# Score tiles of 512 columns in one PSUM bank each, w_out's first piece fetched earlier, and new orders of both stages

## The chip, the cores and the metric

The kernel runs on one core of one Trainium2 chip. The metric is device time in microseconds (us) of one execution, the median of several runs; lower is better. Engines are named as in the profile: PE is TensorE's matmul, PEld its weight load, DVE is VectorE, ACT is ScalarE, POOL is GpSimd, and SP is SyncE, which here only issues DMAs.

## The reference

Three layers follow each other, all in fp32. First bucketed attention: B, H, S, D = 2, 8, 768, 64, and a key counts for a query only where both fall in the same of 64 hash buckets.

```python
q_bits = (np.einsum('bhsd,dk->bhsk', q, proj) > 0); k_bits = ...      # 6 bits
mask = q_bucket[:, :, :, None] == k_bucket[:, :, None, :]
scores = np.where(mask, scale * np.matmul(q, k.transpose(0, 1, 3, 2)), -1e9)
attn = np.exp(scores - scores.max(-1, keepdims=True))
out = np.matmul(attn / (attn.sum(-1, keepdims=True) + 1e-09), v)
```

Then a soft mixture of experts over the 1536 tokens (x is 1536x512, phi 512x32, 8 experts, w1 512x1024, w2 1024x512):

```python
logits = x @ phi
d = softmax(logits, axis=0); c = softmax(logits, axis=1)
slot_input = d.T @ x                                  # 32 slots, 4 for each expert
slot_out[e] = np.maximum(slot_input[e] @ w1[e], 0) @ w2[e]
x = c @ slot_out
```

Last a feed-forward layer: `h = x @ w_in; g = h - np.tanh(h); return g @ w_out`, with w_in 512x2048 and w_out 2048x512. The weights arrive as fp64 and the kernel converts w_in and w_out to fp32 itself.

## The kernel before, in words

**Stage 1, attention (0 to about 263 us).** The 16 heads are worked in 8 pairs (NPR). What each engine does, and in what order, is written out by hand: START lists the units of the beginning, STEP those of one pair (run for pairs 0 to 6), LAST those of pair 7. A unit's name is looked up in `units`, and `role` says for which pair it is done: `m` and `f2` for the next pair, `b` and `h` for the one after it, `s0`, `s1`, `a` for the pair itself, `x2`, `x3`, `lg` for the one before.

- `m` (m_unit, L405) takes 128 queries and all 768 keys of one head: two matmuls (512 and 256 columns) write one PSUM tile `pm`, and DVE takes the row maximum (L412). There are 6 for a head. `f2`, `fa`, `fb` (m_fin) turn the maxima into a row that is added into the scores.
- `s0`, `s1` (s_unit, L461) do 128 keys against all 768 queries of head 0 or 1: four matmuls (L465 and L467, hi and lo parts) write one PSUM tile `pst`, ACT takes the exponential into an SBUF tile `e` (L469), and POOL adds it to the running sum `es` (L474, L480). There are 6 for a head.
- `a` (av_unit, L483) multiplies the two heads' `e` by v into the PSUM tiles `pav` (L492).
- `xr` sums `es` over the partitions with a matmul by ones (L503), `xe` copies `pav` out, `x2` takes the reciprocals, `x3` and `lg` make the tokens and their logits.

All those PSUM tiles (`pm`, `pst`, `pc`, `pb`, `pr`, `pl`, `px` and others) come out of one pool `ps` of three tiles of 768 columns, taken in turn: a new tile waits until the tile three places back has been read. 768 fp32 columns are 3 KB, one bank is 2 KB, so each tile takes two banks. `pav` has two further banks. The `e` tiles are 8 of 768 columns.

**Weights.** `pieces` is the order in which 1 MB pieces are fetched: 32 of w1 and w2, then slots (which = 4, without a DMA) that will hold the converted w_out, and w_out's raw pieces (which = 3). RING says how many slots of SBUF are opened at each of eight points, as buffers of the attention come free; `lp` and `load_pieces` issue the next pieces.

**Stage 2, MOE and feed-forward (263 us to the end).** MOE lists the units of the mixture of experts and of the preparation of the feed-forward layer: `F`, `X`, `y` read the weights, `k` and `i` are matmuls whose result is not used (keep_clock, L748), `ca` to `ce` convert a block f of w_out (ACT L174, DVE L178, L187, L192, ACT L1111, POOL L1112), `m q g s S` make the n-th block of g, `r` and `ra`/`rv` copy the product of the slots with w_in to all rows (L1014, then ACT L1023 or DVE L1021). After MOE all engines load a flag and branch (L1293, L1294); then RUN is worked through, in which `u` stands for three matmuls of 512 columns into an output tile (L1217 to L1219), and a loop (LOOP, LOOP2) does the rest.

Of the kernel before, what the change touches and what calls it, by code (L numbers as in the profile page):

```python
# [10 lines left out]
F32 = mybir.dt.float32  # L11
# [12 lines left out]
NB = 6  # L24
# [103 lines left out]
def body(ctx: ExitStack, tc: tile.TileContext, q, k, v, proj, phi, w1, w2, w_in, w_out, cst, out, dbg=None):  # L128
# [113 lines left out]
    def attention():  # L242
# [9 lines left out]
        e_p = pool("e_p", 8)  # L252
# [11 lines left out]
        ps = actx.enter_context(tc.tile_pool(name="ps", bufs=3, space=PSUM, reuse_waits="tile"))  # L264
# [37 lines left out]
        def psum(name):  # L302
            return ps.tile([P, S], F32, tag="s", name=name)
# [39 lines left out]
        def bits0(i, which):  # L343
            x = (xqs, xks)[which][i]
            pb = psum("pb")
            bt0[which] = e_p.tile([P, S], F32, tag="e", name="bt0")[64:64 + 4 * NB]
            for c0, c1 in ((0, 512), (512, S)):
                nc.tensor.matmul(pb[64:96, c0:c1], projb, x[:, c0:c1], start=True, stop=True, tile_position=(0, 64))  # L348
            for c0, c1 in ((0, 512), (512, S)):
                nc.vector.tensor_scalar(bt0[which][:, c0:c1], pb[64:64 + 4 * NB, c0:c1], 0.0, None, ALU.is_gt)  # L350

        def rows0(i, which, h, eng):
# [3 lines left out]
            for c0, c1, e in {"s": ((0, 512, "a"), (512, S, "v"))}.get(eng, ((0, S, eng),)):  # L356
                y, b = X[i][h][rs, c0:c1], bt0[which][:, c0:c1]
# [47 lines left out]
        def m_unit(i, n):  # L405
            s, h, c = i % 3, n // KT, n % KT
            if i not in mx:
                mx[i] = pre.tile([P, 2 * KT], F32, tag="mx", name="mx")
            pm = psum("pm")
            for c0, c1 in ((0, 512), (512, S)):  # L410
                nc.tensor.matmul(pm[:, c0:c1], QA[s][h][:96, c * P:(c + 1) * P], KA[s][h][:96, c0:c1], start=True, stop=True)  # L411
            nc.vector.reduce_max(mx[i][:, h * KT + c:h * KT + c + 1], pm, axis=AX.X)  # L412

        def m_fin(i, hs=(0, 1)):
            s, n = i % 3, len(hs)
            pc = psum("pc")
            m = pc[:n * KT, :P]
            nc.tensor.transpose(m, mx[i][:, hs[0] * KT:(hs[-1] + 1) * KT], ident)
# [42 lines left out]
        def s_unit(i, h, c):  # L461
            s, t = i % 3, i % 2
            pst = psum("pst")
            for c0, c1 in ((0, 512), (512, S)):
                nc.tensor.matmul(pst[:, c0:c1], KA[s][h][:, c * P:(c + 1) * P], QA[s][h][:, c0:c1], start=True, stop=False)  # L465
            for c0, c1 in ((0, 512), (512, S)):
                nc.tensor.matmul(pst[:, c0:c1], KB[t][h][:, c * P:(c + 1) * P], QB[t][h][:, c0:c1], start=False, stop=True)  # L467
            e = e_p.tile([P, S], F32, tag="e", name="e")
            nc.scalar.activation(e, pst, AF.Exp, scale=0.125)  # L469
            if c == 0:  # L470
                es[i, h, 0] = e
            elif c == 1:
# [873 lines left out]
```

## Time and profile before

| | |
|---|---|
| median of 3 runs | 472.83 us (472.68 to 473.65) |
| profiled execution: time, span | 473.9 us, 472.0 us |
| mean granted clock of PE | 0.984 |
| PE busy | 452.9 us, 96% of the span |
| DVE busy | 325.4 us, 69% |
| POOL busy | 297.5 us, 63% |
| ACT busy | 256.7 us, 54% |

Busy time is the union of an engine's instructions in the trace. Matmuls overlap each other in the records, so a PE that shows 99% busy can still have lost time between two of them; the idle time in front of a weight load, with what ended it, tells more. The windows of the stage table cut the span into the start (13 to 45), the pairs (about 29 us each), the last pair and the tail (235 to 263) and the mixture of experts (263 to 319).

### The profile page before, as it was taken

What the parts mean: (1) busy time and instruction counts of PE and PEld (TensorE: products, weight loads), DVE (VectorE), ACT (ScalarE), POOL (GpSimd) and SP (SyncE); (2) the same over time, 40 slices, a digit from 0 to 9 for tenths busy, and PEclk for the clock granted to TensorE, in tenths of its full rate; (3) what the DMA queues carried; (4) which work ended last, traced back from release to release, by engine and by line L of the source; (5) the groups of instructions that cost most, each with busy time, mean ns of one, the idle gap of its engine ahead of it and who ended that gap; (6) DMA issues with size and microseconds to landing.
All of it is one profiled execution on the core that took longest, in us unless ns stands there. A gap on an engine that the chain in (4) does not pass through costs nothing.

```text
span 472.0 us, 7262 instructions
## 1 busy us (share of the span) xinstructions
PE 452.9 (96%) x2589; PEld 295.7 (63%) x2589; DVE 325.4 (69%) x496; ACT 256.7 (54%) x441; POOL 297.5 (63%) x247
## 2 busy tenths in 40 slices
PE   7799999999999999999999999979999999999995
PEld 3455555655656565565675444547777778888883
DVE  3999688897878969658253658078999976545441
ACT  3434655646556555453452111177798977656661
POOL 3979978789787988679972100025788885353440
PEclk9889999999999999999999999997999999999999
DMA  6337174362834517459589999990000003000003
GB/s 199 109 103 223 56 206 119 104 183 62 231 86 140 145 53 235 183 173 315 228 331 393 316 396 421 419 419 26 1 1 0 0 2 134 2 0 1 0 0 140
DMA packets 18898, 72.66 MB, mean 154 GB/s; under 512 B 3780, under 2 KB 4904, under 8 KB 13736
## 3 DMA queue, kind: packets, MB, share of 16 engines
q1 hardware_dynamic: 18536, 72.12, 44.1%
q8 instruction: 22, 0.36, 0.3%
q14 instruction: 20, 0.16, 0.1%
q10 hardware_dynamic: 320, 0.01, 0.0%
HBM read 60.08 MB, written 3.15 MB: 134 GB/s over the span
## 4 chain that ended last, share of the span: by engine, by line
PE 86%; DVE 8%; ACT 3%; issue 1%; DMA 1%; POOL 0%; SPq 0%; DVEq 0%; ACTq 0%; POOLq 0%
PE pav L492 14%; PE po L1219 9%; PE po L1217 9%; PE po L1218 9%; PE pst L465 8%; PE pm L411 8%; PE pst L467 7%; DVE mx L412 3%; PE po L902 3%; PE ph L1155 2%; PE po L926 2%; PE pl L562 2%; PE pr L503 1%; PE pb L348 1%; ACT e L469 1%; PE px L548 1%
## 5 line engine op out<-in xcount | busy, mean ns | idle before, releaser
L480 POOL TENSOR_TENSOR es<-es,e 128x768 f32<-128x768 f32 x59 | 114.0, 1946 | 13.7 <-ACT e L469 13.5
L469 ACT ACTIVATE e<-pst 128x768 f32<-128x768 f32 x96 | 76.4, 809 | 81.5 <-PE pst L467 77.1
L412 DVE TENSOR_REDUCE mx<-pm 128x1 f32<-128x768 f32 x96 | 87.6, 951 | 13.6 <-PE pm L411 12.5
L492 PE MATMUL pav<-e,tv 128*64 128x256 f32 (+1 forms) x384 | 70.7, 496 | 0.0
L411 PE MATMUL pm<-KA,QA 96*128 96x512 f32 x192 | 53.6, 380 | 5.4 <-DVE mx L412 2.1
L1167 DVE SCALAR_TENSOR_TENSOR ph<-win,ph 128x512 f32<-128x512 f32 x64 | 35.7, 557 | 33.4 <-ACT win L1162 32.2
L465 PE MATMUL pst<-QA,KA 128*128 128x512 f32 x192 | 54.9, 367 | 1.0 <-ACT e L469 0.9
L1198 POOL TENSOR_TENSOR split<-win,split 128x512 fp32r<-128x512 f32 x31 | 44.6, 1440 | 14.1 <-ACT split L1193 12.8
L1219 PE MATMUL po<-w,split 128*128 128x512 f32 x128 | 51.8, 405 | 0.2 <-POOL split L1198 0.2
L1217 PE MATMUL po<-w,split 128*128 128x512 f32 x128 | 51.3, 401 | 0.0
L1218 PE MATMUL po<-w,split 128*128 128x512 f32 x128 | 51.1, 399 | 0.0
L467 PE MATMUL pst<-QB,KB 128*128 128x512 f32 x192 | 49.3, 338 | 0.0
L1198 POOL TENSOR_TENSOR ghl<-win,ghl 128x256 fp32r<-128x256 f32 x32 | 24.4, 763 | 38.4 <-ACT ghl L1193 38.4
L492 PEld LDWEIGHTS pav<-e,tv 128*64 128x64 f32 x384 | 24.5, 136 | 38.1 <-issue 36.4
L411 PEld LDWEIGHTS pm<-KA,QA 96*128 96x128 f32 x192 | 29.5, 192 | 29.4 <-ACT e L469 10.3
L474 POOL TENSOR_TENSOR es<-e 128x768 f32<-128x768 f32 x16 | 34.5, 2159 | 20.0 <-ACT e L469 19.9
L1162 ACT ACTIVATE win<-ph 128x512 f32<-128x512 f32 (+1 forms) x64 | 30.8, 481 | 24.7 <-PE ph L1155 24.0
L1168 DVE SCALAR_TENSOR_TENSOR win<-win,ph 128x512 f32<-128x512 f32 x64 | 35.5, 554 | 8.3 <-ACT win L1163 0.2
L1163 ACT ACTIVATE win<-win,ct 128x512 f32<-128x512 f32 (+1 forms) x64 | 39.5, 617 | 2.1
L465 PEld LDWEIGHTS pst<-QA,KA 128*128 128x128 f32 x192 | 29.0, 189 | 14.3 <-issue 6.4
L467 PEld LDWEIGHTS pst<-QB,KB 128*128 128x128 f32 x192 | 29.4, 188 | 4.2
L1219 PEld LDWEIGHTS po<-w,split 128*128 128x128 f32 x128 | 24.4, 191 | 8.2 <-POOL split L1198 3.0
(233 smaller groups left out, 785.8 us busy)
## 6 DMA issues: line engine op xcount, KB each, us to landing
w<-in_moe_w_dram SPq DMA_DIRECT2D x32, 1024.0 KB
raw<-in_moe_w_in_dram SPq DMA_DIRECT2D x16, 512.0 KB
w<-in_moe_w_out_dram SPq DMA_DIRECT2D x8, 1024.0 KB
xq<-in_q_dram SPq DMA_DIRECT2D x8, 384.0 KB
xk<-in_k_dram SPq DMA_DIRECT2D x8, 384.0 KB
tv<-in_v_dram SPq DMA_DIRECT2D x8, 384.0 KB
out_dram<-win SPq DMA_DIRECT2D x12, 256.0 KB
QB<-QA SPq DMA_DIRECT2D x10, 192.0 KB
```

The lines of the kernel that those rows point to most:

```text
L411: nc.tensor.matmul(pm[:, c0:c1], QA[s][h][:96, c * P:(c + 1) * P], KA[s][h][:96, c0:c1], start=True, stop=True)
L412: nc.vector.reduce_max(mx[i][:, h * KT + c:h * KT + c + 1], pm, axis=AX.X)
L465: nc.tensor.matmul(pst[:, c0:c1], KA[s][h][:, c * P:(c + 1) * P], QA[s][h][:, c0:c1], start=True, stop=False)
L467: nc.tensor.matmul(pst[:, c0:c1], KB[t][h][:, c * P:(c + 1) * P], QB[t][h][:, c0:c1], start=False, stop=True)
L469: nc.scalar.activation(e, pst, AF.Exp, scale=0.125)
L480: eng.tensor_tensor(es[i, h][0], es[i, h][0], e, ALU.add)
L492: nc.tensor.matmul(pav[i][j][64 * h:64 * h + 64, :], tv[i][:, h, c, :], e2[h][:, c0:c1], start=False, stop=c == KT - 1, tile_position=(0, ...
L1163: nc.scalar.activation(w, z, AF.Square, bias=ct[:, C_QA:C_QA + 1])
L1198: (eng or nc.gpsimd).tensor_tensor(gl[p], g, gh[p].bitcast(F32), ALU.subtract)
L1217: nc.tensor.matmul(po, gh[p][:, us], wo.half(f, 0), start=f == 0, stop=False)
L1218: nc.tensor.matmul(po, gh[p][:, us], wo.half(f, 1), start=False, stop=False)
L1219: nc.tensor.matmul(po, gl[p][:, us], wo.half(f, 0), start=False, stop=f == NF - 1)
```

## The change

PSUM tiles of `ps` have 512 columns, one bank, and there are six. A head's 6x768 scores are now cut into 9 units of 512 columns (SEQ): six take columns 0 to 511 of one chunk of 128, three take columns 512 to 767 of two chunks, side by side. So there are 9 `m` for a head (maxima in two tiles, joined by one more DVE instruction in m_fin) and 9 `s`, 9 `a` for a pair. The sums `es` are two tiles for a head, and the one of the paired units is folded by one more POOL instruction. `e` tiles are 12 of 512. `x3` uses two tiles. In the last pair the last two `e` of a head are summed by `xr` itself, which now has three column ranges. RING has one slot more at its sixth point. w_out's first raw piece and its slot stand before the last piece of w2. START, STEP, LAST, MOE and RUN are new lists. Cut to its core:

```diff
+SEQ = ((0,), (1,), (0, 1), (2,), (3,), (2, 3), (4,), (5,), (4, 5))
-RING, HOLD = (4, 2, 2, 4, 3, 1, 3, 1), 4
+RING, HOLD = (4, 2, 2, 4, 3, 2, 3, 1), 4
+    pieces[-1:-1] = [(3, 0, 0), (4, 0, 0)]
     for which in (4, 3):
-        for n in range(8):
+        for n in range(1, 8):
-        e_p = pool("e_p", 8)
+        e_p = pool("e_p", 12)
-        ps = actx.enter_context(tc.tile_pool(name="ps", bufs=3, space=PSUM, reuse_waits="tile"))
+        ps = actx.enter_context(tc.tile_pool(name="ps", bufs=6, space=PSUM, reuse_waits="tile"))
-            return ps.tile([P, S], F32, tag="s", name=name)
+            return ps.tile([P, 512], F32, tag="s", name=name)
         def m_unit(i, n):
+            c0, c1 = PARTS[len(cs) - 1]
+            for j, c in enumerate(cs):
+                nc.tensor.matmul(pm[:, j * 256:j * 256 + c1 - c0], QA[s][h][:96, c * P:(c + 1) * P], KA[s][h][:96, c0:c1], start=True, stop=True)
+            m = mx[i][len(cs) - 1][:, h * KT + cs[0]:h * KT + cs[-1] + 1]
+            nc.vector.reduce_max(m, pm.rearrange("p (c k) -> p c k", c=len(cs)), axis=AX.X)
         def m_fin(i, hs=(0, 1)):
+            nc.vector.tensor_tensor(mh[0], mh[0], mh[1], ALU.max)
         def s_unit(i, h, n):
+            for j, c in enumerate(cs):
+                for K, Q, x in ((KA[s], QA[s], 0), (KB[t], QB[t], 1)):
+                    nc.tensor.matmul(pst[:, j * 256:j * 256 + c1 - c0], K[h][:, c * P:(c + 1) * P], Q[h][:, c0:c1], start=x == 0, stop=x == 1)
+            e = e_p.tile([P, 512], F32, tag="e", name="e")
             nc.scalar.activation(e, pst, AF.Exp, scale=0.125)
+            if end and n >= len(SEQ) - 2 or not q:
+                q.append(e)
+            else:
+                eng.tensor_tensor(q[0], y, e, ALU.add)
+                if n == len(SEQ) - 1:
+                    nc.gpsimd.tensor_tensor(q[0][:, :256], q[0][:, :256], q[0][:, 256:], ALU.add)
         def xr(i):
+            for x in range(3):
+                o, w, a, k = ((0, HALF, 0, 0), (0, 512 - HALF, HALF, 0), (512 - HALF, 256, 0, 1))[x]
+                for n in range(4):
+                    for h in range(2):
...
+                            g = 2 * h + min(x, 1)
+                            nc.tensor.matmul(pr[32 * g:32 * g + 32, o:o + w], ones32, q[n], start=n == 0, stop=n == len(q) - 1,
+                                             tile_position=(0, 32 * g))
         def x3(i):
+            for c0, c1 in ((0, 4), (4, KT)):
+                px = psum("px")
-STEP = ("s0 m a xe m s1 l1 lp s0 xr m m s1 l0 s0 m v m v1 m a wl e m h1 d s1 m l2 wl m wl m h3 s0 a a lp wc wl l3 lp e "
+STEP = ("a a a m m m a l1 s0 m s1 s0 m xe m s0 m s1 l0 xr h1 m m m s0 m s1 a m m v wl l2 v1 m s1 s0 a wc lp m s0 m a d "
```

Three places of the order, before and then with the change. On DVE in the start: the maxima of pair 0 (`mx<-pm`, of head 0 and, after `zrow` and `row`, of head 1). Before:

```order
L412 TENSOR_REDUCE mx<-pm 128x1 x8
L421 TENSOR_SCALAR zrow<-pc 6x128
L422 SCALAR_TENSOR_TENSOR row<-zrow,pc 6x128
L412 TENSOR_REDUCE mx<-pm 128x1 x4
L178 TENSOR_SCALAR cl<-raw 128x512
```

With the change (two maxima of single chunks, one of a pair, and so on, 9 of them in front of `zrow`; then the new joining instruction):

```order
L421 TENSOR_REDUCE mx<-pm 128x1 x2
L421 TENSOR_REDUCE mx<-pm 128x2
L426 TENSOR_TENSOR mx<-mx 128x6
L432 TENSOR_SCALAR zrow<-pc 6x128
L433 SCALAR_TENSOR_TENSOR row<-zrow,pc 6x128
```

Eight reductions of 768 columns stood ahead of `zrow`, now nine of 512 and one instruction on 6 columns; nine more follow where four did.

On PE inside a pair: a piece from an `a` on (`pav`), with the score tiles that follow it. Before:

```order
L492 MATMUL pav<-e,tv 64x512 x2
L492 MATMUL pav<-e,tv 64x256 x2
L411 MATMUL pm<-KA_132,QA_128 128x512
L411 MATMUL pm<-KA_132,QA_128 128x256
L465 MATMUL pst<-QA_131,KA_135 128x512
L465 MATMUL pst<-QA_131,KA_135 128x256
L467 MATMUL pst<-QB_136,KB_139 128x512
L467 MATMUL pst<-QB_136,KB_139 128x256
```

With the change:

```order
L501 MATMUL pav<-zrw,vzw 128x256
L507 MATMUL pav<-e,tv 64x256 x4
L507 MATMUL pav<-e,tv 64x512 x2
L478 MATMUL pst<-QA_131,KA_135 128x512
L478 MATMUL pst<-QB_136,KB_139 128x512
L419 MATMUL pm<-KA_132,QA_128 128x512
L478 MATMUL pst<-QA_131,KA_135 128x256
L478 MATMUL pst<-QB_136,KB_139 128x256
```

(The last two rows come once more, for the second chunk of the paired unit.) The columns of a pair are the same, but they come in 36 units of 512 instead of 24 of 768; the runs of `pav` between them are 6 in a pair instead of 5.

On PE at the end of MOE, around the branch: `po<-hold,selr` and `po<-hl,selr` are the `r` units, `po<-ct` a matmul without use, L1217 to L1219 the first `u`. Before:

```order
L750 MATMUL po_2649<-ct 128x256
L1293 TENSOR_LOAD flag
L1294 COMPARE_AND_BRANCH
L1014 MATMUL po_2652<-hold_2765,selr 128x256
L1014 MATMUL po_2652<-hl,selr 128x256
L1014 MATMUL po_2651<-hold_2765,selr 128x256
L1014 MATMUL po_2651<-hl,selr 128x256
L1217 MATMUL po_2647<-w,split 128x512
```

With the change (L774 is L750, L1246 to L1248 are L1217 to L1219, L1038 is L1014):

```order
L774 MATMUL po_3033<-ct 128x256 x4
L1322 TENSOR_LOAD flag
L1323 COMPARE_AND_BRANCH
L1246 MATMUL po_3031<-w,split 128x512
L1247 MATMUL po_3031<-w,split 128x512
L1248 MATMUL po_3031<-w,split 128x512
L1038 MATMUL po_3036<-hold_3151,selr 128x256
L1038 MATMUL po_3036<-hl,selr 128x256
```

Four matmuls without use instead of one stand ahead of the branch, and the first `u` stands ahead of the last two `r`.

## Rows read from the trace of the kernel before

**Rows 1.** Stage table: busy us of each engine (instructions), granted clock, DMA share, GB/s.

```profile
core 0: us, PE busy (x) PEld busy (x) DVE busy (x) ACT busy (x) POOL busy (x), PEclk, DMA share, GB/s
13.00:45.00 32.00, 28.71 (x126) 16.85 (x126) 30.72 (x41) 13.11 (x18) 28.96 (x27) 0.89 0.50 143
92.00:121.00 29.00, 28.84 (x167) 17.25 (x163) 24.06 (x33) 16.77 (x25) 24.00 (x17) 1.00 0.46 136
209.30:235.00 25.70, 25.65 (x150) 15.73 (x146) 15.55 (x20) 9.60 (x14) 23.55 (x17) 1.00 0.81 266
263.00:319.00 56.00, 52.35 (x488) 26.34 (x488) 33.44 (x53) 15.29 (x36) 6.35 (x15) 0.98 0.98 397
```

**Rows 2.** PE in time order, 103.5 to 106.7: start, us, what.

```profile
104.70 0.51 PE L467 MATMUL pst<-QB,KB 128*128 128x512 f32 x2
105.06 0.51 PE L465 MATMUL pst<-QA,KA 128*128 128x512 f32 x2
105.41 0.51 PE L467 MATMUL pst<-QB,KB 128*128 128x512 f32 x2
```

**Rows 3.** Weight loads in time order, 92 to 106, with the idle time before.

```profile
93.65 0.30 PEld L465 LDWEIGHTS pst<-QA,KA 128*128 128x128 f32 x2 [0.32 <-DVE mx L412]
95.58 0.30 PEld L411 LDWEIGHTS pm<-KA,QA 96*128 96x128 f32 x2 [0.37 <-ACT e L469]
```

**Rows 4.** Waits of the weight loads, 62 to 235: us in total, times, longest.

```profile
PEld pm L411 <- ACT e L469: 8.4, 23, 0.6
PEld pst L465 <- DVE mx L412: 3.1, 12, 0.3
PEld pm L411 <- DVE mx L412: 2.6, 8, 0.4
```

**Rows 5.** Groups by line and shape: busy us, mean ns | idle before.

```profile
L412 DVE TENSOR_REDUCE mx<-pm 128x1 f32<-128x768 f32 x96 | 87.6, 951 | 13.6 <-PE pm L411 12.5
L1167 DVE SCALAR_TENSOR_TENSOR ph<-win,ph 128x512 f32<-128x512 f32 x32 | 22.2, 695 | 33.4 <-ACT win L1162 32.2
L1167 DVE SCALAR_TENSOR_TENSOR ph<-win,ph 128x256 f32<-128x256 f32 x32 | 13.4, 420 | 0.0
L552 DVE TENSOR_TENSOR xtok<-px,rs 128x768 f32<-128x768 f32 x7 | 6.7, 958 | 9.8 <-PE px L548 9.8
L528 DVE RECIPROCAL rs<-rs 128x12 f32<-128x12 f32 x8 | 1.8, 228 | 0.3
L469 ACT ACTIVATE e<-pst 128x768 f32<-128x768 f32 x96 | 76.4, 809 | 81.5 <-PE pst L467 77.1 <-issue 2.1 <-PE pav L492 2.0
L1162 ACT ACTIVATE win<-ph 128x512 f32<-128x512 f32 x32 | 19.1, 597 | 24.5 <-PE ph L1155 23.9
L480 POOL TENSOR_TENSOR es<-es,e 128x768 f32<-128x768 f32 x59 | 114.0, 1946 | 13.7 <-ACT e L469 13.5
L474 POOL TENSOR_TENSOR es<-e 128x768 f32<-128x768 f32 x16 | 34.5, 2159 | 20.0 <-ACT e L469 19.9
L1198 POOL TENSOR_TENSOR split<-win,split 128x512 fp32r<-128x512 f32 x31 | 44.6, 1440 | 14.1 <-ACT split L1193 12.8 <-DVE win L187 1.4
L1198 POOL TENSOR_TENSOR ghl<-win,ghl 128x256 fp32r<-128x256 f32 x32 | 24.4, 763 | 38.4 <-ACT ghl L1193 38.4
```

**Rows 6.** DVE in time order, 13 to 31.

```profile
13.16 7.01 DVE L412 TENSOR_REDUCE mx<-pm 128x1 f32<-128x768 f32 x8 [0.77 <-PE pm L411]
20.60 3.53 DVE L412 TENSOR_REDUCE mx<-pm 128x1 f32<-128x768 f32 x4
```

**Rows 7.** Chain of waits, 245 to 256: start, us, what.

```profile
250.73 1.43 PE pr L503 x16
```

**Rows 8.** PE in time order, 315 to 324.

```profile
315.94 0.70 PE L750 MATMUL po<-ct 128*128 128x256 f32 x2
318.32 0.58 PE L1014 MATMUL po<-hold,selr 32*128 32x256 f32 x2 [1.69 <-DVE hold L1021]
319.05 0.80 PE L1217 MATMUL po<-w,split 128*128 128x512 f32 x1
```

**Rows 9.** Stage table of all engines at the branch; columns as in the first.

```profile
316.80:323.50 6.70, 5.17 (x15) 4.01 (x16) 6.56 (x12) 4.19 (x9) 3.17 (x3) 0.50 0.38 155
323.60:330.30 6.70, 6.70 (x32) 5.50 (x31) 5.68 (x8) 6.35 (x14) 3.62 (x3) 1.00 0.00 0
```

More of the change, by code (lines that the diff above doesn't have):

```diff
@@ L344, in bits0 @@
             x = (xqs, xks)[which][i]
[L345 to L350, printed above, removed]
+            w = (512, S - 512)
+            bt0[which] = [e_p.tile([P, 512], F32, tag="e", name="bt0")[64:64 + 4 * NB, :n] for n in w]
+            pbs = [psum("pb") for _ in w]
+            for j, (c0, c1) in enumerate(((0, 512), (512, S))):
+                nc.tensor.matmul(pbs[j][64:96, :w[j]], projb, x[:, c0:c1], start=True, stop=True, tile_position=(0, 64))
+            for j in range(2):
+                nc.vector.tensor_scalar(bt0[which][j], pbs[j][64:64 + 4 * NB, :w[j]], 0.0, None, ALU.is_gt)
         def rows0(i, which, h, eng):
@@ L355, in rows0 @@
             w = ct[rs, o:o + 2]
-            for c0, c1, e in {"s": ((0, 512, "a"), (512, S, "v"))}.get(eng, ((0, S, eng),)):
-                y, b = X[i][h][rs, c0:c1], bt0[which][:, c0:c1]
+            for (c0, c1), b, e in zip(((0, 512), (512, S)), bt0[which], "av" if eng == "s" else 2 * eng):
+                y = X[i][h][rs, c0:c1]
                 if e == "a":
@@ L459, in v_unit2, with s_unit @@
             vz[i] = vzw
[L461 to L462 removed]
+        def s_unit(i, h, n):
+            s, t, cs = i % 3, i % 2, SEQ[n]
+            k, (c0, c1) = len(cs) - 1, PARTS[len(cs) - 1]
             pst = psum("pst")
[L464 to L468, printed above, removed]
[L469 to L481 removed]
@@ new lines, in s_unit, with av_unit @@
+            return e
+        def av_unit(i, n, e2):
+            cs = SEQ[n]
+            k, (c0, c1) = len(cs) - 1, PARTS[len(cs) - 1]
+            if cs[0] == 0:
+                if k == 0:
+                    pav[i] = [pav_p.tile([P, w], F32, tag=f"pav{w}", name="pav") for w in (512, S - 512)]
+                nc.tensor.matmul(pav[i][k], vz[i], zr[i].rearrange("r c j -> r (c j)")[:, c0:c1], start=True, stop=False,
+                                 skip_group_check=True)
+                if k == 1:
+                    del zr[i], vz[i]
+            for j, c in enumerate(cs):
+                for h in ((k + j) % 2, (k + j + 1) % 2):
+                    nc.tensor.matmul(pav[i][k][64 * h:64 * h + 64, :], tv[i][:, h, c, :], e2[h][:, j * 256:j * 256 + c1 - c0],
@@ L633, in s_next @@
             c = half.get((i, h), 0)
-            if c == KT:
+            if c == len(SEQ):
                 return
@@ L709, in attention @@
                     open_ring(RING[2], rctx)
-                if i == last and half.get((i, 0)) == KT and len(slots) == sum(RING[:4]) and not xtu and last in pav:
+                if i == last and half.get((i, 0)) == len(SEQ) and len(slots) == sum(RING[:4]) and not xtu and last in pav:
                     head_x.close()
@@ L714, in attention @@
                     load_pieces(RING[4])
-                if i == last and half.get((i, 1)) == KT and len(slots) == sum(RING[:5]):
+                if i == last and half.get((i, 1)) == len(SEQ) and len(slots) == sum(RING[:5]):
                     last_x.close()
```

110 lines of the change are left out of this document (50 added, 60 removed), and 9 rows, old and new, of tables (MOE, START).

## The prediction, made before the change was timed

> **What bounds the kernel now.** I read the stage table first, then the time order of PE in one pair, then the waits of its weight loads, then the groups by shape for the prices. In the stage table [rows 1] PE is busy for 28.84 of 29.0 us in a middle pair, DVE for 24.06, POOL for 24.00, ACT for 16.77, and the clock is 1.00: PE sets the pace of the pairs, and no other engine is within 4 us of it. Only in the start, 13 to 45, is another engine the fuller one: DVE is busy for 30.72 of 32 us. In the mixture of experts PE has 52.35 of 56 us and the DMA share is 0.98.
>
> A busy PE still loses time, and the second view shows where. Where nothing waits, a pass of 768 columns follows the next after 0.35 to 0.36 us (104.70, 105.06, 105.41) [rows 2]. Elsewhere the weight load of a new score tile stands still for 0.32 or 0.37 us until DVE's maximum or ACT's exponential has read an older tile [rows 3]: the tile three places back. Between 62 and 235, six pairs, such waits add up to 8.4 us for ACT and 3.1 + 2.6 us for DVE, 14.1 us in 43 waits [rows 4], so 2.35 us of a pair of 28.9. That is the most that a longer rotation can give back.
>
> **Part 1: the rotation, in the pairs.** PE's own work does not change: the same columns of `pm`, `pst` and `pav`, in 36 units of 512 instead of 24 of 768. The wait was for the third tile back, with 0.81 or 0.95 us [rows 5] to read it; it is now for the sixth back, with about 0.60 or 0.70 us. Three units of 768 are 2304 columns ahead, six of 512 are 3072, a third more, and the reading is a quarter shorter. The waits for ACT are the larger half and ACT is 58% busy, so it is not late by its load but only by its delay; these I expect to go almost wholly. Those for DVE come from its queue (w_in's conversion, the lo parts) and can outlast six units; half of them stay. Value: 7.4 of 8.4 and 2.8 of 5.7, so 10.2 of 14.1 us, 1.7 us a pair. Against it stands one more run of `pav` in a pair and two switches of PE between it and score tiles; no row isolates a switch, so I bound it by zero and by the longest weight-load wait, 0.6 us [rows 4], and take 0.3 to 0.4. Net gain 1.3 us a pair; for six pairs 7.8 us. Bounds: 0 and 14.1.
>
> **What the cover costs.** The other engines get more instructions, which is hidden only while PE stays the longest.
> - DVE: 18 reductions of 512 for 12 of 768. No row has that reduction, so the nearest is a DVE instruction that reads 512 columns of PSUM, 695 ns [rows 5]: 18 x 0.695 - 12 x 0.951 = +1.10 us. The joining maximum costs about the 0.23 us of the small reciprocal, and `x3` in two parts 0.695 + 0.420 - 0.958 = +0.16. Sum +1.5: 24.1 becomes 25.6 us of a pair.
> - ACT: 18 x 0.597 - 12 x 0.809 = +1.0, to 17.8.
> - POOL: ten adds at a mean of (114.0 + 34.5) / 75 = 1.98 us, 19.8, become 14 of 512 and two of 256. By the split's rows that is 14 x 1.44 + 2 x 0.763 = 21.7, by the columns alone 19.8. Between the two: +1.0, to 25.0.
>
> With PE at 28.9 - 1.3 = 27.6 us all three stay below it, DVE by 2 us. Next late is DVE: if all waits went, PE would need 26.5 to 26.9, and DVE's 25.6 leaves no room for its own waits.
>
> The price of one more instruction is the point where the skill can be set against the trace. The rows give, from 768 to 512 columns, (951 - 695) / 256 = 1.0 ns a column and 183 ns that do not depend on columns [rows 5]. The Trainium skill, Perfetto Trace Analysis, section Optimizing Scalar/DVE Operations, puts the fixed part of a DVE instruction on PSUM at about 125 ns, and says that grouping helps a saturated engine while splitting helps one that is not saturated but makes others wait. By its figure six more reductions would be 0.75 us instead of 1.1, and DVE would stand at about 25.2 us; the trace's rows are dearer.
>
> **Part 2: the start and pair 0.** Here DVE is the bound. Eight maxima take 7.01 and four 3.53 us back to back, 0.88 each [rows 6]; scaled by 695 / 951, one of 512 takes 0.64. For pair 0: 18 x 0.64 - 12 x 0.88 = +1.0 us, and 0.2 for the two joins. The same comes for pair 1's maxima up to 45 us, where the new tiles give something back. The other split instructions are of 24 rows and lie on ACT and POOL beside it. Bounds +0.5 and +2.5; I take +1.5.
>
> **Part 3: the tail.** In the last pair `xr` does two rounds of 384 columns on four column tiles, 1.43 us, on the chain [rows 7]: 1.86 ns a column. Now one column tile of a head has 2 x 128 + 4 x 256 = 1280 columns and the other 768. If they run beside each other from the start it takes 2.4 us, if the first round stands ahead of it 3.1: +0.95 to +1.7. I take +1.3. Everything else in the tail is the same work.
>
> **Part 4: the end of MOE.** PE's last matmul ahead of the branch starts at 315.94, and PE is idle for 1.69 us before 318.32 [rows 8]. The clock stands at 0.50 (1.2 GHz) from 316.8 to 323.5, and at 1.00 after it [rows 9]. The `u` matmuls begin at 319.05, so 4.4 us of them run at half the clock and about 2.2 us are lost. Four unused matmuls now fill the idle time, and the first `u` needs no `r`. All engines wait there for the same flag, so the branch itself is not earlier. If the clock stays high, PE gains those, but ACT (6.56 of 6.70) and then DVE and ACT (5.68, 6.35) are next [rows 9]. Bounds 0 and -2.5; I take -0.8. The weights: the DMA share is 0.98 [rows 1], w2's last piece now comes one piece later, and one more slot is opened before it. A piece of 1.05 MB at 397 GB/s is 2.6 us; between -0 and +2.6, and 0 taken, since the two cancel.
>
> **Sum.** +1.5 - 7.8 + 1.3 - 0.8 = -5.8 us. The profiled execution took 473.9 us with a span of 472.0, 0.2% above the median of 472.83. Off the median: 467.0 us. About 0.2%, 1 us, is what can be told from no change.
>
> **Rivals.**
> 1. All waits go. PE's rows speak for it (the waits are short, most are for ACT), DVE's load against. 14.1 - 6 x 0.35 = 12.0 instead of 7.8 in the pairs, and -1.5 at the branch: 472.83 - 12.0 + 1.5 + 1.3 - 1.5 = 462 us. Chance 0.16.
> 2. DVE becomes the bound beyond the start: slower. The place is the start and the first pairs, where w_in is converted too; it decides if DVE's present idle time (4.9 us of a pair) do not shrink with PE's, so that 25.6 + 4.9 exceeds 28.9. Price: 2.5 us up to pair 0, 0.6 us of net loss in each of pairs 1 to 3, nothing gained after, +1.3 in the tail, -0.5 at the branch: +5, that is 478; half of it, where the later pairs gain something, is 475.5. Speaks for it 30.72 of 32 [rows 1]; against it the 24.06 of 29 after that. By the skill's section named above, grouping for a saturated engine, it would be this case. Chance 0.17.
> 3. The change doesn't do what it says: with half as many again tiles to wait for, the waits only move. Pairs gain 0.4 each, 2.4 in all, which start, tail and branch (+2.0) eat: 472.4. Chance 0.11.
> 4. The weights come late: PE reaches the mixture of experts sooner than DMA can follow, at 0.98 share. Then up to 2.6 us of the gain come back: 469.6. Against it: the slots open as the attention frees them, so the stream moves with it. Chance 0.10.
>
> **How the numbers follow.** The forecast has 0.46, with a range of its own from 464 to 470. Faster by over 0.2%: 0.46 + 0.16 + 0.10 and a little of rival 3, 0.73. Within 0.2%: 0.10. Slower: 0.17. The range reaches from 459.5 (under rival 1, with nearly all of part 4's bound) to 476 (the milder half of rival 2).
>
> **What would show it.** Right: in a middle pair the period is 27 to 28 us, the waits of weight loads for ACT's exponential between pairs 1 and 6 fall from 8.4 to about 1 us, DVE shows 25 to 26 us of a pair, maxima of 512 near 0.7 us. The first exponential comes about 1 us later than before. `xr` in the tail shows 2.4 to 3.1 us. The clock at the branch shows whether part 4 pays. Wrong: a period of 28.5 or more, or DVE's reductions at 0.8 us; POOL's adds over 1.5 us with exponentials waiting for them; or PE waiting for a DMA in the mixture of experts.

## The result, and the profile after

The changed kernel took 476.74 us (median of 20 runs, 475.33 to 481.11), the kernel before 473.52 us in 20 runs beside it: a ratio of 1.0075, 95% interval 1.0053 to 1.0097. It is slower by 0.75%, where 467.0 us and a gain had been forecast. The profiled execution took 475.81 us with a span of 473.8. The median of before lay between 473.45 and 474.23 us in the sets of runs below; each experiment's ratio is against the runs of before beside it.

The stage table of the changed kernel, columns as in [rows 1]:

```profile
13.00:45.00 32.00, 25.25 (x114) 16.71 (x114) 29.98 (x51) 13.09 (x22) 27.73 (x30) 0.84 0.53 155
92.00:121.00 29.00, 27.02 (x159) 16.76 (x159) 24.61 (x39) 15.98 (x29) 24.95 (x23) 0.94 0.44 135
209.30:235.00 25.70, 25.70 (x154) 16.47 (x153) 19.03 (x31) 11.51 (x22) 20.39 (x18) 1.00 0.72 221
263.00:319.00 56.00, 53.97 (x535) 28.42 (x534) 32.83 (x56) 11.74 (x27) 3.88 (x13) 1.00 1.01 416
```

In the middle pair PE is busy for 27.02 of 29 us, not 28.84, and the mean clock is 0.94, not 1.00. So PE now stands still, and then works slowly for a while. The waits of PE between 62 and 235 say where (engine, tile, line, what it waited for: us in total, times, longest):

```profile
PE pc L429 <- DVE mx L426: 8.2, 5, 2.0
```

`pc` is the transpose of the row maxima in `f2`, and L426 is the new joining maximum (the join, for short). PE, DVE and POOL in time order around one such place (start, us, what):

```profile
106.86 1.08 PE L507 MATMUL pav<-e,tv 128*64 128x512 f32 x4
109.91 0.28 PE L429 MATMUL pc<-ct,mx 128*12 128x128 f32 x1 [1.98 <-DVE mx L426]
```

```profile
105.57 1.91 DVE L408 TENSOR_TENSOR QB<-xq,QB 64x768 fp32r<-64x768 f32 x1
107.41 1.27 DVE L421 TENSOR_REDUCE mx<-pm 128x1 f32<-128x512 f32 x2
108.71 0.28 DVE L465 TENSOR_TENSOR vt<-pv,blk 4x128 f32<-4x128 f32 x1
108.92 0.94 DVE L426 TENSOR_TENSOR mx<-mx 128x12 f32<-128x12 f32 x1
```

```profile
105.37 1.29 POOL L490 TENSOR_TENSOR es<-es,e 128x512 f32<-128x512 f32 x1
106.63 1.98 POOL L490 TENSOR_TENSOR es<-e 128x512 f32<-128x512 f32 x1
108.57 1.25 POOL L490 TENSOR_TENSOR es<-es,e 128x512 f32<-128x512 f32 x1
```

PE has nothing to do for 1.98 us. DVE is never idle in that time: it reaches the join late, and the join, 12 numbers a partition, takes 0.94 us. POOL's add that was under way ends at 109.82, the join at 109.86. The same holds for all seven joins of 12 columns: each ends 0.02 to 0.04 us after the POOL add into which it fell, and takes 0.16 us where that add was nearly over (pair 7) and 0.83 to 0.95 us elsewhere. `L408` (unit `l3`) ahead of it also has two SBUF inputs, and takes 1.91 us where it took 0.95 in the middle pairs of before, there L401:

```profile
105.92 0.95 DVE L401 TENSOR_TENSOR QB<-xq,QB 64x768 fp32r<-64x768 f32 x1
```

After the wait the clock falls. Three windows of the changed kernel, columns as in the stage table:

```profile
110.80:114.20 3.40, 3.40 (x17) 2.43 (x15) 1.88 (x5) 2.51 (x4) 3.32 (x5) 0.50 0.49 182
141.50:144.90 3.40, 3.40 (x15) 2.31 (x13) 1.78 (x4) 2.25 (x4) 3.32 (x5) 0.50 0.51 185
172.20:175.60 3.40, 3.40 (x18) 2.02 (x10) 1.59 (x5) 1.91 (x4) 3.32 (x5) 0.50 0.14 53
```

PE works for 3.4 us at 1.2 GHz behind three of the four waits of 1.94 to 2.00 us, and so loses 1.7 us each time. (Behind the first of the four, 2.00 us up to 80.56, the clock stays; no run shows why.) The periods from `pc` to `pc` show both: 27.7, 29.35, 30.84, 30.88, 29.74 and 28.89 us, where before had 28.1, 28.8, 28.9, 28.9, 29.3 and 29.9. From pair 1's `pc` to pair 7's it is 177.4 us, before 173.9.

The groups that answer to [rows 5] and the waits of weight loads that answer to [rows 4]:

```profile
L421 DVE TENSOR_REDUCE mx<-pm 128x1 f32<-128x512 f32 x96 | 63.3, 682 | 7.7 <-PE pm L419 7.2
L480 ACT ACTIVATE e<-pst 128x512 f32<-128x512 f32 x144 | 81.0, 597 | 84.2 <-PE pst L478 80.4 <-PE pav L507 2.0
L490 POOL TENSOR_TENSOR es<-es,e 128x512 f32<-128x512 f32 x73 | 93.0, 1287 | 3.4 <-ACT e L480 3.3
```

```profile
PEld pc L429 <- DVE mx L426: 11.4, 4, 2.9
PEld pm L419 <- ACT e L480: 7.3, 12, 0.8
PEld pm L419 <- DVE mx L421: 4.9, 6, 0.8
```

The prices of the split instructions were right (0.68, 0.60, 1.29 us; the 30 adds that open a sum took 1.60). The loads' waits for ACT hardly fell, but what PE spends did: from each start to the next, summed over a middle pair, `pm` takes 4.66 us where it took 5.81, and `pst` 9.77 where it took 9.93, although some of that pair's scores ran at half clock (8.95 us in experiment 2, where none did).

At the branch, [rows 8] and [rows 9], PE in time order and the window behind it:

```profile
320.41 1.99 PE L774 MATMUL po<-ct 128*128 128x256 f32 x8
322.05 0.58 PE L1246 MATMUL po<-w,split 128*128 128x512 f32 x1
```

```profile
319.50:326.20 6.70, 6.33 (x32) 4.42 (x33) 6.14 (x16) 6.06 (x15) 3.36 (x4) 1.00 0.81 333
```

There the clock stays at 1.00 and PE has 6.33 us of work in 6.7.

### The profile page after: what moved, and what is told of

It is laid out like the page before. It is cut to its first block, busy times and chain, and to the rows that moved or that the text cites. A ratio compares the mean times of both kernels' runs of the same rounds, so it can differ in the third digit from the quotient of the medians.

```text
span 473.8 us, 7576 instructions
## 1 busy us (share of the span) xinstructions
PE 445.7 (94%) x2639; PEld 300.4 (63%) x2639; DVE 336.0 (71%) x564; ACT 260.6 (55%) x493; POOL 300.7 (63%) x291
## 5 line engine op out<-in xcount | busy, mean ns | idle before, releaser
L480 ACT ACTIVATE e<-pst 128x512 f32<-128x512 f32 x144 | 81.0, 597 | 84.2 <-PE pst L478 80.4
L421 DVE TENSOR_REDUCE mx<-pm 128x1 f32<-128x512 f32 x144 | 90.0, 681 | 9.2 <-PE pm L419 8.7
L490 POOL TENSOR_TENSOR es<-es,e 128x512 f32<-128x512 f32 x73 | 93.0, 1287 | 3.4 <-ACT e L480 3.3
L507 PE MATMUL pav<-e,tv 128*64 128x512 f32 (+1 forms) x384 | 72.7, 500 | 0.1
L490 POOL TENSOR_TENSOR es<-e 128x512 f32<-128x512 f32 x30 | 47.7, 1599 | 31.2 <-PE pr L521 27.9
L478 PE MATMUL pst<-QA,KA 128*128 128x256 f32 (+1 forms) x192 | 67.2, 363 | 0.0
L478 PE MATMUL pst<-QB,KB 128*128 128x256 f32 (+1 forms) x192 | 64.2, 346 | 0.0
L1196 DVE SCALAR_TENSOR_TENSOR ph<-win,ph 128x512 f32<-128x512 f32 (+1 forms) x64 | 35.7, 558 | 32.6 <-ACT win L1191 31.2
L1248 PE MATMUL po<-w,split 128*128 128x512 f32 x128 | 51.0, 398 | 0.0
L1246 PE MATMUL po<-w,split 128*128 128x512 f32 x128 | 50.6, 396 | 0.0
L478 PEld LDWEIGHTS pst<-QA,KA 128*128 128x128 f32 x192 | 37.4, 195 | 19.6 <-issue 10.4
L1197 DVE SCALAR_TENSOR_TENSOR win<-win,ph 128x512 f32<-128x512 f32 (+1 forms) x64 | 35.5, 555 | 8.3 <-ACT win L1192 0.2
L1248 PEld LDWEIGHTS po<-w,split 128*128 128x128 f32 x128 | 24.0, 188 | 7.7 <-POOL split L1227 2.7
```

Of the source, the lines that this page charges most:

```text
L421: nc.vector.reduce_max(m, pm.rearrange("p (c k) -> p c k", c=len(cs)), axis=AX.X)
L478: nc.tensor.matmul(pst[:, j * 256:j * 256 + c1 - c0], K[h][:, c * P:(c + 1) * P], Q[h][:, c0:c1], start=x == 0, stop=x == 1)
L490: eng.tensor_tensor(q[0], y, e, ALU.add)
L507: nc.tensor.matmul(pav[i][k][64 * h:64 * h + 64, :], tv[i][:, h, c, :], e2[h][:, j * 256:j * 256 + c1 - c0], start=False, stop=c == KT - 1 ...
L1196: nc.vector.scalar_tensor_tensor(self.ph[p], z, Q_C, self.ph[p], ALU.mult, ALU.mult)
L1246: nc.tensor.matmul(po, gh[p][:, us], wo.half(f, 0), start=f == 0, stop=False)
```

## The experiments

Each was timed beside before. Ratios are those of the runs, with 95% intervals.

**1. Fill PE's wait.** In m_fin, for pairs 2 to 5:

```diff
             pc = psum("pc")
+            if 2 <= i <= 5:
+                keep_clock(pc, 4)
```

> The changed kernel, with four unused matmuls of 256 columns into pc in front of the transpose of the maxima (L429), for pairs 2 to 5 only: 4 x 0.35 us of work where PE stands idle for 1.94 to 2.00 us. Theory (PE waits at pc, and the half clock follows from that idle time): the three stretches of 3.4 us at 0.5 (from 110.8, 141.5 and 172.2) vanish, 3 x 1.7 us come back, so about 471.6 us against 476.7 of the changed kernel. The wait itself stays, 0.5 us behind the fillers. Rival 1 (the low clock comes from something else, such as the shorter units): the stretches stay, 476.7 us. Rival 2 (DVE's load sets the length of these pairs): PE runs faster into the next wait, 475 to 477 us.

Measured: 472.16 us, ratio 0.9968 (0.9946 to 0.9989). The window of the middle pair:

```profile
92.00:121.00 29.00, 28.80 (x174) 18.41 (x174) 25.99 (x42) 16.44 (x30) 24.94 (x23) 1.00 0.48 136
```

All three stretches at half clock are gone, and 4.6 us with them. The theory holds: with work in place of the idle time the clock stays at 1.00, and the low clock costs the changed kernel 4 to 5 us.

**2. A join of one input.**

```diff
-                mx[i] = [pre.tile([P, 2 * KT], F32, tag=f"mx{j}", name="mx") for j in range(2)]
+                mt = pre.tile([P, 2, 2 * KT], F32, tag="mx", name="mx")
+                mx[i] = [mt[:, 0, :], mt[:, 1, :], mt]
...
-            nc.vector.tensor_tensor(mh[0], mh[0], mh[1], ALU.max)
+            mj = pre.tile([P, 2 * KT], F32, tag="mxj", name="mxj")[:, :n * KT]
+            nc.vector.reduce_max(mj, mx[i][2][:, :, hs[0] * KT:(hs[-1] + 1) * KT].rearrange("p t c -> p c t"), axis=AX.X)
```

> The changed kernel, with the two sets of maxima in one tile of two planes and joined by one maximum along the planes (one input) in place of the maximum of two tiles. Theory (the join takes 0.94 us because it reads two SBUF inputs while POOL adds; 0.16 us where POOL does not): the join falls to about 0.2 us in all nine places, PE's idle time at pc from about 2.0 to 1.25 us in five pairs, and the half clock after it in some or all: 468 to 473 us. Rival 1 (DVE is held for another reason, whatever the form of the instruction): 0.9 us as before, 476.7 us. Rival 2 (DVE's load sets the pairs): the join is short, but the period of pairs 2 to 5 falls by no more than 0.2 us: 475.5 to 476.7 us.

Measured: 469.27 us, ratio 0.9888 (0.9854 to 0.9922), 7.5 us below the changed kernel. DVE, POOL and PE in time order at the same place:

```profile
106.21 0.15 DVE L427 TENSOR_REDUCE mxj<-mx 128x12 f32<-128x24 f32 x1
```

```profile
105.86 3.74 POOL L491 TENSOR_TENSOR es<-es,e 128x512 f32<-128x512 f32 x3
```

```profile
106.42 0.28 PE L430 MATMUL pc<-ct,mxj 128*12 128x128 f32 x1 [1.18 <-DVE mxj L427]
```

In the middle of POOL's adds the join now takes 0.15 us. PE still waits 1.2 us in four pairs, but no stretch at half clock follows. The theory holds: it is the second SBUF input that waits for POOL. The edit changes the kind of instruction too, from a TENSOR_TENSOR to a reduction, but the kind alone does not explain it: `vt<-pv,blk`, a TENSOR_TENSOR with one input in PSUM and one in SBUF, starts at 108.71 inside the same POOL add as the join of the changed kernel and takes 0.28 us, what it also takes in before with no POOL add beside it.

**3. f2 two runs of `a` later.**

```diff
-... wl a h3 lp f2 b wl s0 lp wc h2 s1 x2 kc wc e a a s1 lg x3 fz lp
+... wl a h3 lp b wl s0 lp h2 s1 a a f2 x2 wc kc wc e s1 lg x3 fz lp
```

> The changed kernel, with f2 (join, transpose, row) moved in STEP behind two runs of a that stood after it, and one conversion wc behind f2 instead of ahead. Theory (PE waits for DVE's join only because f2 stands too close behind the last maxima): PE is idle at pc for under 0.3 us, the half clock is gone, the period of pairs 2 to 5 falls from 29.4 to 30.9 us to 27.5 to 28.5: 463 to 468 us. Rival 1 (DVE's load sets the pairs): the same idle time shows at the next score tile or row, and the period stays over 29 us: 474 to 477 us. Rival 2 (too late): the row of f2 comes after the scores of the next pair want it, and PE waits there for more than 1 us a pair: 470 to 474 us.

Measured: 476.37 us, ratio 1.0027 (0.9996 to 1.0058). No wait at `pc` is left, but the waits of PE show another:

```profile
PE pst L478 <- DMA QA<-row: 8.0, 5, 3.1
```

Rival 2 was right in its mechanism, and its bounds too low; the theory's were wrong by 8 us or more. Nor is the half clock gone, as the theory had it: there are two stretches of it in the pairs, from 64.5 and 153.3.

**4. The second stage alone**, on the tiles and orders of before (new MOE, RUN, pieces, and RING's sixth point).

> The kernel before with the changed second stage alone: new MOE and RUN, w_out's first piece ahead of w2's last, one slot more at the sixth point; the score tiles and START, STEP and LAST as before. Theory (the second stage gains by itself what the traces show, 3.3 us up to the first u and 1.2 after it, the clock at the branch staying at 1.00): 469 to 470 us, against 473.5 of the kernel before. Rival 1 (the gain came only from a later start of the mixture of experts, with the weights further ahead): PE waits for DMA there, 472.5 to 475 us. Rival 2 (half of it: the branch gains, the part before it does not): 471.5 us.

Measured: 468.67 us, ratio 0.9882 (0.9855 to 0.9910). F.0 starts at 264.49 us (before 264.58), the first `u` at 314.34 (319.05), PE's last matmul 5.6 us sooner after F.0. No stretch at half clock is left between 26 and 465 us. The window of [rows 9], by its times:

```profile
316.80:323.50 6.70, 6.34 (x29) 4.93 (x28) 6.36 (x12) 5.82 (x14) 4.64 (x4) 1.00 0.05 22
```

**5. The first stage alone**, on the second stage of before.

> The changed kernel with the second stage of before (its MOE, RUN, order of pieces and ring): the score tiles and START, STEP, LAST alone. Theory (the two stages add up: the new second stage alone gave 473.96 - 468.67 = 5.3 us): 476.7 + 5.3 = 482 us, and F.0 starts near 271 us. Rival (the later weights or the tail's extra work belong together, so that the second stage's gain came only with the new first stage, or the reverse): 477 us or less.

Measured: 479.98 us, ratio 1.0155 (1.0138 to 1.0172), so +6.5 us; F.0 at 270.47. That is 2 us under the 482 expected, and 3 us over the rival's bound. The two parts, +6.5 and -5.3, make +1.2 where +3.2 was measured; the difference of 2.0 us is at the edge of what the three intervals leave open (half-widths of 0.8, 1.3 and 1.0 us). So these times neither show nor exclude that the parts act on each other.

**6. f2 one score unit later**, and **7.** the same with the join of one input.

```diff
-... wl a h3 lp f2 b wl s0 lp wc h2 s1 ...
+... wl a h3 lp b wl s0 lp f2 wc h2 s1 ...
```

> The changed kernel, with f2 in STEP one score unit later (behind b, wl and s0, but still ahead of the runs of a), the join as it is. With f2 behind two runs of a, the row came late by its DMA: PE waited 8.0 us in five pairs for it. Theory (there is a place between the two waits): PE idle at pc falls from 1.9 to 2.0 us to 0.3 to 0.7 us, the row arrives in time, no stretch at half clock: 476.7 - 5 x 1.4 - 4.5 = 465 us, 463 to 468. Rival 1 (the row is late here too): waits for the row's DMA of over 1 us a pair, 470 to 476 us. Rival 2 (DVE is late by its queue, and what is taken from pc shows at the next score tile): waits of pst or pm for DVE of over 1 us a pair, 470 to 476 us.

> The changed kernel with both: the join of one input, and f2 one score unit later. Theory: PE's 1.2 us of idle time at pc that the join of one input left in five pairs goes too, the period of the middle pairs is 27.4 us (28.55 less 1.17): 469.3 - 5 x 1.2 = 463 us, 462 to 465. Rival (the rest of the wait moves to the next tile that wants DVE): period 28.0 to 28.6, 467 to 469.5 us.

Measured: 474.33 us, 1.0012 (0.9992 to 1.0033), and 473.40 us, 1.0003 (0.9977 to 1.0028). The first lies in the range of both rivals, and its trace has a part of each: PE waits 2.8 us at `pc`, 3.1 us for the row's DMA, and 1.5 us at the scores for DVE's maxima. The second lies above both of its ranges; it is 4 us slower than experiment 2, from which it differs only by the later f2. PE waits 6.1 us in it for the row's DMA.

**8. Four PSUM tiles instead of six**, with the join of one input (`bufs=6` to `bufs=4`).

> The changed kernel with the join of one input, and four PSUM tiles of 512 columns in ps in place of six: 2048 columns ahead, less than the 2304 of before. This asks whether the longer rotation gave what the prediction put down to it (1.7 us a pair; in the traces the score tiles of a pair take 4.66 + 8.95 us of PE's time where they took 5.81 + 9.93). Theory (the number of tiles in turn gives it): the score tiles go back to 15 us or more a pair, the period to 29.5 to 31: 476 to 485 us. Rival (smaller tiles that are read sooner give it, whatever their number): under 14 us a pair for the score tiles, 469 to 471 us.

Measured: 485.48 us, ratio 1.0262 (1.0236 to 1.0287), 16 us above experiment 2. The middle pair takes 30.85 us instead of 28.55, and the waits of PE show

```profile
PE pst L479 <- ACT e L481: 7.4, 15, 0.5
```

From each start to the next `pm` now takes 6.9 us and `pst` 9.7 in a middle pair, more than the 5.81 and 9.93 of before. So it is the number of tiles in turn that gives the time, as the prediction had it; smaller tiles alone do not.

**9. The join alone, in the kernel before.**

```diff
+            t = mx[i][:, hs[0] * KT:(hs[-1] + 1) * KT]
+            nc.vector.tensor_tensor(t, t, t, ALU.max)
             pc = psum("pc")
```

> The kernel before with one more DVE instruction in m_fin, ahead of the transpose: the maximum of the row maxima with themselves (two SBUF inputs, the same numbers come out). Nothing else is changed. It asks what the joining maximum costs by itself, on the path of pc. In before the transpose follows its neighbours on PE with no idle time, and DVE's last maximum ends 0.25 us ahead of it. Theory (PE waits for the small instruction, and it for POOL's add, which takes about 2 us there): PE idle at pc 0.6 to 1.8 us in each of the pairs, with or without half clock after it: 473.5 + 4 to 11 us, so 477 to 485. Rival 1 (the join is hidden by DVE's 4.9 us of idle time in a pair): 473 to 474 us. Rival 2 (POOL is not adding at that point in this order, so that the join takes 0.16 us): 474 to 475.5 us.

Measured: 479.77 us, ratio 1.0118 (1.0081 to 1.0155). DVE and POOL in time order, and the waits of PE from 62 to 235:

```profile
109.71 0.81 DVE L417 TENSOR_TENSOR mx<-mx 128x12 f32<-128x12 f32 x1
```

```profile
108.16 4.10 POOL L482 TENSOR_TENSOR es<-es,e 128x768 f32<-128x768 f32 x2 [0.97 <-ACT e L471]
```

```profile
PE pc L420 <- DVE mx L417: 4.4, 6, 1.3
```

The first of the two POOL adds ends at 110.48, the join at 110.52. An instruction of 12 columns, seven times and twice at half width, makes the kernel 5.5 us longer. PE's waits here are 0.66 us in a middle pair, and no stretch at half clock follows in the pairs.

**10. l3 and qk behind f2 and b**, with the join of one input.

```diff
-a lp e l3 wl e qk a s1 m lp ... wl a h3 lp f2 b wl s0 lp wc
+a lp e wl e a s1 m lp ... wl a h3 lp f2 b l3 qk wl s0 lp wc
```

> The changed kernel with the join of one input, and with l3 (the low part of q, 1.91 us on DVE of which 1.0 us is spent until POOL's add ends) and the loads qk that follow it moved in STEP from ahead of the last maxima to behind f2 and b. f2 and its DMA keep their place. Theory (DVE comes late to the join by its queue): the join comes up to 1.9 us earlier, PE's remaining 1.2 us of idle time at pc goes in five pairs, the period of the middle pairs is 27.4 to 27.7 us: 462.5 to 465 us. Rival 1 (what l3 needs behind f2 is missed there: the first s1 of the next pair waits for it): PE waits for DVE's QB, 468 to 474 us. Rival 2 (the wait moves to the next tile that wants DVE): 467 to 470 us.

Measured: 466.45 us, ratio 0.9812 (0.9763 to 0.9860). No wait at `pc` in the pairs, and no other of note took its place; five middle periods are 26.3 to 27.9 us, three of them 27.34 or 27.35. The median is 1.5 us above the range expected; its profile starts 3.8 us later than that of experiment 2 (`pc` of pair 0 at 20.87 instead of 17.08), and one of its six runs took 461.47 us (see the end).

**11. w_in's load behind f2**, on experiment 7 (`b wl s0 lp f2 wc` to `b s0 f2 wl lp wc`; `lp`, the next weight pieces, moves too).

> The changed kernel with the join of one input, f2 behind b and one s0 as in the last run, but the load of w_in's next raw piece (wl, 512 KB) behind f2 in place of ahead of it. In that run the middle pairs took 28.4 to 29.2 us, with PE idle for 0.6 to 1.4 us at the first scores of a pair, for the row's DMA. Theory (the small DMA of the row stood behind the large one in the queue of SP): PE's waits for the row fall under 0.2 us a pair, the period to 27.8 to 28.2: 465 to 468 us. Rival (the row is late because of the DMAs that b issues, or DVE reads the maxima too late anyway): as the last run, 471 to 474 us.

Measured: 473.16 us, ratio 0.9972 (0.9947 to 0.9997). PE still waits 5.5 us for the row's DMA: the rival was right, I had moved the wrong load. SP's issues in experiment 3 (start, us, what) show which DMAs stand ahead of the row:

```profile
115.28 1.64 SPq L157 DMA_DIRECT2D KA<-rt  x2
116.97 1.48 SPq L157 DMA_DIRECT2D QA<-rt  x2
118.50 1.47 SPq L157 DMA_DIRECT2D KA<-rt  x2
120.02 1.47 SPq L157 DMA_DIRECT2D QA<-rt  x2
121.59 0.73 SPq L157 DMA_DIRECT2D QA<-row  x1
```

The eight `rt` DMAs belong to `b`, which stood ahead of f2 in experiments 3, 6, 7 and 11.

**12. As 10, but the join of two inputs.**

> The changed kernel with l3 and qk behind f2 and b as in the last run, but with the join of two SBUF inputs as in the changed kernel. It asks which of the two makes PE wait: the join's own length, or DVE's queue ahead of it. Theory (DVE's queue: l3 stood 1.91 us ahead of the join, more than the 1.94 to 2.00 us of idle time less a few hundredths): the join may still take 0.9 us or so, but it starts 1.9 us earlier, PE is idle at pc for 0 to 0.3 us, no stretch at half clock, the middle pairs take 27.4 to 27.7 us: 466 to 468.5 us. Rival (the join's wait for POOL's add moves with it, and PE waits 0.5 to 1.2 us in each pair, perhaps with half clock): 470 to 475 us.

Measured: 465.59 us, ratio 0.9829 (0.9802 to 0.9857). DVE in time order:

```profile
105.72 0.69 DVE L421 TENSOR_REDUCE mx<-pm 128x2 f32<-128x512 f32 x1 [0.15 <-PE pm L419]
106.41 0.28 DVE L465 TENSOR_TENSOR vt<-pv,blk 4x128 f32<-4x128 f32 x1
106.62 0.76 DVE L426 TENSOR_TENSOR mx<-mx 128x12 f32<-128x12 f32 x1
```

DVE now waits for PE ahead of the last maximum, not the reverse. The join still takes 0.76 us, and PE waits 0.14 us for it at most in pairs 2 to 7. The middle period is 27.5 us, and the median 0.4 us under the range expected. So the place of `l3` alone, one instruction of DVE with a DMA pair (`qk`), decides between 476.7 and 465.6 us. Either cure is enough against the half clock: a short join (experiment 2) or a DVE that gets there sooner (this one); both together (experiment 10) give no more than this one.

**13. f2 one s0 later, but ahead of b**, with the join of one input (`f2 b wl s0 lp wc` to `s0 f2 b wl lp wc`).

> The changed kernel with the join of one input and f2 one s0 later, as two runs before, but with f2 ahead of b. In the three runs with f2 later it also stood behind b, and in their traces the row, ready on DVE, is issued by SP only 6 us later, behind the eight DMAs of b's rt rows (1.47 to 1.64 us for two). Theory (that queue, and not the later place, made the row late): SP issues the row right behind DVE's row, no PE wait for it, idle time at pc 1.2 us less one s0 (0.5 to 0.6) or less, the middle pairs 27.4 to 28.0 us: 463 to 467 us. Rival (a later f2 is bad by itself, because PE catches up with DVE's maxima): 28.4 to 29 us a pair, 470 to 474 us.

Measured: 466.23 us, ratio 0.9852 (0.9821 to 0.9882). SP's issue of the row:

```profile
107.99 0.82 SPq L157 DMA_DIRECT2D QA<-row  x1
109.52 1.56 SPq L157 DMA_DIRECT2D KA<-rt  x2
```

The row leaves ahead of b's DMAs, PE waits for it nowhere in the pairs, and 0.33 to 0.35 us remain at `pc`; the middle pairs take 28.2 to 28.3 us, a little over what was expected. So what made f2's later place bad in experiments 6, 7 and 11 was SP's queue; for experiment 3, where f2 stands later still, only the rows of SP say so. Experiments 10, 12 and 13 are 7.6 to 8.4 us faster than before and 10 to 11 us faster than the changed kernel; the runs don't tell them apart.

## Why the prediction was wrong, point by point

**Part 1, what it gains: right in size.** The forecast was -7.8 us for the six pairs. Where PE doesn't wait for the join, the stretch from pair 1's `pc` to pair 7's is 165.8 us (experiment 12) or 165.1 (experiment 10), against 173.9 of before: -8.1 and -8.8. Experiment 8 shows that the longer rotation is the reason. The terms fit too: in a middle pair of experiment 12 `pm` and `pst` take 2.1 us less than before from start to start and `pav` 0.4 us more (forecast 1.7, and 0.3 to 0.4). But the sign by which it was to be seen was wrong: the weight loads' waits for ACT were to fall from 8.4 to about 1 us and are 7.3, and 6.5 in experiment 12, where the gain is whole. A load can wait while PE still works on the matmuls before it, and in PE's own list of waits none of these stands; what the matmuls take from start to start would have been the view.

**Part 1, what the cover costs: the step that failed.** "The joining maximum costs about the 0.23 us of the small reciprocal", and "all three stay below it, DVE by 2 us". That counted the join as load of DVE. But it stands between the last maxima and a transpose that PE meets at once in its order, so what counts is when DVE gets there. Three things were missed. DVE is late there by its queue: `l3` stands ahead of it with 1.91 us (experiment 12). The join takes 0.94 and not 0.23 us, since POOL adds at that time (experiments 2 and 9). And behind the idle time the clock falls (experiment 1). Together they turn -8 into +3.5 us.

The trace of before had a sign of it that [rows 4] leaves out. In the same view, waits of weight loads from 62 to 235, the load of that transpose already waits for DVE's last maximum in five of the six pairs, so whatever is put between the two comes on top:

```profile
PEld pc L418 <- DVE mx L412: 1.9, 5, 0.4
```

The loads themselves were priced a little high: 18 x 0.682 - 12 x 0.951 = +0.86 us for DVE's reductions, forecast +1.10. With the measured 682 ns the two sizes give 1.05 ns a column and 144 ns beside it, not 1.0 and 183, which had been worked out from two kinds of instruction.

On the second of the three: the join begins at 108.92, inside POOL's add of 108.57 to 109.82, and ends 0.04 us behind it. The Trainium skill, SBUF — State Buffer, section SBUF: two separate sides, states it: a DVE instruction with two SBUF inputs and a GpSimd one that reads SBUF exclude each other for the whole instruction. The traces agree, with 0.94 us for two inputs and 0.15 us for one.

**Rival 2** had the time, 478 or 475.5 us, and a part of the reason (DVE's idle time doesn't shrink), but put it down to DVE's load in the start and the first pairs. The load isn't it: in experiment 12 DVE does the same work in 27.5 us. And the loss came in other places than it said: the two periods from pair 3's `pc` to pair 5's lose most, 1.9 and 2.0 us, where it had 0.6 a pair at most and none behind pair 3, and the second stage gave nearly 4 us more than its -0.5. That its sum came near 476.7 is luck.

**Part 2: mis-sized.** Experiment 4 has the old first stage in an execution that starts like that of the changed kernel (its first score tiles at 11.08 and 10.90 us). Up to pair 1's `pc` the changed kernel is 52.88 - 49.63 = 3.25 us later; the forecast was 1.5, at most 2.5. Of it 1.34 us are PE's wait for pair 1's join, so again the failed step; the other 1.9 us lie between the 1.5 and the bound. The first exponential comes at 33.89 instead of 30.27 us, not 1 us later as forecast.

**Part 3: the term a little too high.** The last `xr` takes 2.3 us from its start to the next `pav`, instead of 1.43: +0.9, just under the lower bound of 0.95 (forecast 1.3). PE in time order, before and then with the change:

```profile
250.66 0.85 PE L503 MATMUL pr<-es,ones 128*32 128x384 f32 x8
252.09 2.80 PE L492 MATMUL pav<-e,tv 128*64 128x512 f32 x16
```

```profile
255.16 0.52 PE L521 MATMUL pr<-es,ones 128*32 128x384 f32 x6
257.48 3.66 PE L507 MATMUL pav<-e,tv 128*64 128x256 f32 x24
```

From its start to F.0 there are 17.0 us, before 13.9. Three more unused matmuls now stand ahead of F.0; in experiment 4, which has them too and the old tail, it is 15.2 us. So they are 1.3 us and this stretch lost 1.8. What `xr` doesn't explain of it, 0.9 us, is `pav`, by these rows: 24 matmuls behind `xr` where 16 stood. That is work which the new order moved from ahead of `xr`, not new work.

**Part 4: mis-sized, and the bound wrong.** The forecast was -0.8, at best -2.5; the second stage alone gave -5.3 us. By the traces of experiment 4 and before, PE takes 196.1 instead of 201.7 us from F.0 to its last matmul. The three more unused matmuls ahead of F.0 cost 1.3 of that (part 3), so 4.3 are gained. PE's idle time went from 3.8 to 1.6 us, and the 5.17 us that ran at half clock [rows 9] now run at full, worth 2.6. The prediction had seen both, but its bound of -2.5 has room for the clock alone, and of that it thought ACT and DVE would take back most; they didn't. It also misread a row there: of the 6.70 us, 6.56 is DVE's, and ACT has 4.19. The weights were late nowhere: PE waited for no DMA in that stage.

So the sum, in the traces, against the old first stage: +3.25 up to pair 1's `pc`, +2.6 from there to the last `xr`, +1.8 in the tail, -4.3 in the second stage: +3.4, and +3.2 was measured. With the join off PE's path (experiments 10, 12 and 13) the kernel takes 465.6 to 466.5 us, inside the 464 to 470 of the forecast; that it is under 467.0 and not over it is part 4. One figure of the range does not come out: with all of part 4's bound rival 1 gives 461.1 us, and the 1.6 us down to 459.5 have no term.

## What to carry to other kernels

A new instruction between two engines is priced by when its engine gets to it, not by its load: look up in the trace what stands ahead of it on its engine, and whether the waiting engine has other work. A wait can move to a DMA queue when a unit is moved past another that issues DMAs, so every such move is followed on SP too. A small DVE instruction with two SBUF inputs can be held until the POOL instruction beside it ends, 0.94 us for 12 columns in most places of the changed kernel and 1.63 at most (experiment 9); one tile and a reduction along it (0.15 us) avoid that.

## What the runs showed of the hardware that was not expected

- A DVE maximum of 12 columns with two SBUF inputs took 0.15 to 1.63 us in the experiments, by where in a POOL add it began; with one input 0.15 to 0.17 us in the pairs.
- Behind PE's idle times of 1.94 to 2.00 us the granted clock fell to 0.50 (1.2 GHz) in three of four places, and in experiment 5 behind 1.96 to 1.99 us again in three of four; behind 1.16 to 1.20 us (experiment 2) and 0.66 us (experiment 9) in none. The length alone doesn't decide: in experiment 3 the clock fell behind 3.09 and 1.41 us and not behind 1.75.
- The start differs from one profiled execution to the next, with the same START list too. In the profile of before the first four matmuls of `pb` take 2.74 us, in that of the changed kernel 1.45 us (PE in time order, one row of each):

```profile
6.23 2.74 PE L348 MATMUL pb<-xk,projb 128*32 128x512 f32 x4
```

```profile
6.78 1.45 PE L355 MATMUL pb<-xk,projb 128*32 128x512 f32 x4
```

  The first score tile follows at 12.54 and 10.90 us. With the START of before it comes at 11.08 in experiment 4; with that of the changed kernel at 10.45 in experiment 5, and at 13.6 to 13.9 in experiments 3, 7, 10 and 11. That is up to 3.5 us which no edit of START made, and no run shows the cause; only medians of several runs, or stretches of the traces behind it, can be compared to less.
